# A decode block on one core: the first K in halves, longer weight runs, two quads of heads per PSUM bank, and y formed as rows

## The chip, the cores and the metric

The kernel runs on one core of a Trainium2 chip. The metric is the device time of one execution, in microseconds (us). Each kernel was run several times; the text quotes medians, and where the trace is read, the span of the profiled run (first to last instruction, about 1.8 us less than the device time).

## The reference, cut to what matters

One decode step for two sequences: layer norm, attention of 32 heads over a cache of 8,192 positions, a residual, a second layer norm, a gated MLP and another residual.

```python
# x [2,1,512]; k_cache, v_cache [2,32,8192,128]; wq [512,4096]; wo [4096,512]  (bf16)
q = layernorm(x) @ wq                              # 32 heads of 128
p = softmax(q . k * 128**-0.5);  o = p . v         # per head
h = x + o @ wo
g = layernorm(h) @ W_gate;  u = layernorm(h) @ W_up   # 512 -> 1376
h2 = h + ((g * (g > 0)) * u) @ W_down
```

K and V are 134 MB each; the weights are about 12.6 MB. The arithmetic is small, so the caches have to stream past once.

## The kernel before

A quad is four heads of one sequence; there are 16 quads. VectorE multiplies K with q and adds it up by halving, ScalarE makes the exponentials, TensorE multiplies them with V. K has a ring of two buffers and V one buffer, so a load can be issued only when its buffer has been read.

```python
def scores(n):                       # VectorE: one multiply, four halvings, one reduction
    nc.vector.tensor_tensor(out=kt, in0=kt, in1=q_broadcast, op=ALU.mult)
    ...
load_k(0); load_k(1); load_v(0)
for n in range(N - 1):
    scores(n)
    load_k(n + 2)                    # waits until scores(n) has read its buffer
    weighted_v(n)                    # TensorE
    load_v(n + 1)                    # waits until weighted_v(n) has read the buffer
# --- the end: wo, last V in four parts, gate, up (3/4 and 1/4), down
...
mlp_in(0, gate_ps, 0, KC)            # 44 matmuls of 2 columns
mlp_in(1, up_ps, 0, KC - 1)          # 33, need the first up transfer only
mlp_in(1, up_ps, KC - 1, KC)         # 11, need the second
...                                  # act = relu(gate) * up
for fc in range(FC):                 # y in columns: 44 matmuls of 2 columns
    for c in range(KC):
        nc.tensor.matmul(out=y_ps[:, c, :], lhsT=wd[:, fc][:, c * P:(c + 1) * P], rhs=act[:, fc, :], ...)
nc.vector.tensor_tensor(out=y, in0=y_ps, in1=hc, op=ALU.add)
...                                  # four transposes on TensorE, two copies, one output transfer
```

The softmax here doesn't subtract the row's maximum and nothing guards it: scores larger than these inputs give would overflow.

## Time and profile before

| | before |
|---|---|
| device time, median of 3 | 662.81 us |
| span of the profiled run | 660.9 us |
| bytes moved, share of the DMA engines' time in the kernel's queue | 281.28 MB, 98.9% |
| VectorE busy | 588.0 us (89%) |

The page of the kernel before, cut to its span, the busy times (us, share of the span, instructions), the kernel's queue (packets, MB, share of 16 engines' span) and the chain of waits:

```profile
span 660.9 us, 3558 instructions
...
PE 135.1 (20%) x1478; PEld 66.0 (10%) x1481; DVE 588.0 (89%) x139; ACT 74.4 (11%) x204; POOL 10.6 (2%) x51
...
q1 hardware_dynamic: 8244, 281.06, 98.9%
...
DVE 60%; DMA 36%; SPq 3%; issue 0%; PE 0%; DVEq 0%
```

Two engines look full. The queue is the one that is: VectorE still waits for K, while the queue holds its rate. The windows view has, for each stretch, the busy time and number of instructions of PE, PEld, DVE, ACT and POOL, then the granted clock, the DMA share and GB/s:

```profile
69.00:109.00 40.00, 7.83 (x72) 3.29 (x74) 39.76 (x8) 7.30 (x20) 0.00 (x0) 0.59 0.98 420
109.00:288.00 179.00, 35.40 (x365) 15.89 (x364) 177.77 (x32) 18.10 (x52) 0.00 (x0) 0.60 1.00 433
...
644.00:655.00 11.00, 8.57 (x171) 8.30 (x172) 2.04 (x14) 1.12 (x4) 0.00 (x0) 0.55 0.99 381
```

The stream runs at 433 GB/s in the middle. It is slower around the third K, at 69 to 109 us, and at the end, where the weights load.

Two lines of the timeline (start, duration, engine, line, operation) show why at 69 us: VectorE can start only when the whole first K has landed, and the third K is issued (SPq is the queue's issuing engine) only when the first has been read. By then the queue is nearly empty.

```profile
32.85 17.23 DVE L202 TENSOR_TENSOR k<-k,qrep 128x32768 bf16<-128x32768 bf16 x1 [23.45 <-DMA k<-in_A_k_cache_dram]
...
69.19 0.33 SPq L187 DMA_DIRECT2D k<-in_A_k_cache_dram  x1
```

The timeline of the end: the V matmuls of the second part of the last V, hd (h minus its mean), the up matmuls, act, the y matmuls in two lots, the last copy and the output:

```profile
642.62 1.26 PE L238 MATMUL o<-v,pm 128*16 128x512 bf16 x20 [1.96 <-DMA v<-in_A_v_cache_dram]
...
650.60 0.16 DVE L417 TENSOR_TENSOR hd<-hc,ln2mu 128x8 bf16<-128x8 f32 x1 [0.68 <-PE ln2mu L126]
...
652.83 1.71 PE L431 MATMUL up_ps<-hd,W 128*128 128x2 bf16 x44
...
654.58 0.24 DVE L452 TENSOR_TENSOR act<-gate,up_ps 96x2 bf16<-96x2 f32 x2 [0.94 <-PE up_ps L431]
...
654.87 0.57 PE L459 MATMUL y_ps<-act,W 128*128 128x2 bf16 x16 [0.33 <-DVE act L452]
...
656.24 1.09 PE L459 MATMUL y_ps<-act,W 128*128 128x2 bf16 x24 [0.80 <-DMA W<-in_B_W_down_dram]
...
658.38 0.41 DVE L476 CAST y_row<-yt_ps 2x256 bf16<-2x256 f32 x1 [0.75 <-PE yt_ps L470]
658.87 0.32 SPq L477 DMA_DIRECT2D out_dram<-y_row  x1
```

The gap between the two lots of y matmuls is a wait for W_down, as the view of waits says (who waited, for what, us, times, longest):

```profile
PE y_ps L459 <- DMA W<-in_B_W_down_dram: 0.8, 1, 0.8
```

### The profile page before, as it was taken

How to read it: one execution, taken by the hardware profiler on the slowest of the kernel's cores; microseconds unless marked ns; L12 is line 12 of the kernel's file. 1: busy time of each engine (PE TensorE's matmuls, PEld its weight loads, DVE VectorE, ACT ScalarE, POOL GpSimd, SP SyncE). 2: the span in 40 equal slices, each digit the busy share in tenths (PEclk: the TensorE clock that was granted, in tenths of full speed). 3: DMA queues.
4: the chain of work that ended last, by engine and by line, in shares of the span. 5: the costliest groups of instructions: out<-in, count | busy, mean ns of one | idle time of the engine just before them, and what ended most of it. 6: DMA issues, size and time to landing. Idle time of an engine off the chain costs nothing.

```text
span 660.9 us, 3558 instructions
## 1 busy us (share of the span) xinstructions
PE 135.1 (20%) x1478; PEld 66.0 (10%) x1481; DVE 588.0 (89%) x139; ACT 74.4 (11%) x204; POOL 10.6 (2%) x51
## 2 busy tenths in 40 slices
PE   2100402104040220304012030401204040130446
PEld 1000100001020010101001010100102010010215
DVE  1099999999999999999999998989899998999931
ACT  2100201010100101010102001010100101011020
POOL 6000000000000000000000000000000000000000
PEclk9755655757565575756657575565757556575765
DMA  9999999999999999999999999999999999999996
GB/s 381 444 444 440 386 444 440 441 444 405 428 437 441 440 409 433 445 432 436 440 420 429 444 425 436 440 424 432 429 436 436 440 425 437 424 428 440 400 410 251
DMA packets 8264, 281.28 MB, mean 426 GB/s; under 512 B 724, under 2 KB 1336, under 8 KB 3768
## 3 DMA queue, kind: packets, MB, share of 16 engines
q1 hardware_dynamic: 8244, 281.06, 98.9%
q8 instruction: 11, 0.18, 0.1%
q14 instruction: 5, 0.04, 0.0%
q10 hardware_dynamic: 4, 0.00, 0.0%
HBM read 281.05 MB, written 0.00 MB: 425 GB/s over the span
## 4 chain that ended last, share of the span: by engine, by line
DVE 60%; DMA 36%; SPq 3%; issue 0%; PE 0%; DVEq 0%
DMA k<-in_A_k_cache_dram 29%; DVE k L202 29%; DVE k L207 28%; DMA W<-in_A_wo_dram 5%; DVE sc L211 4%; SPq L364 3%; DMA W<-in_B_W_down_dram 2%; DVE ou L278 0%; DVE rep L275 0%; PE yt_ps L470 0%; PE y_ps L459 0%; DVE y_row L476 0%; SPq L119 0%; SPq L352 0%; DVEq L211 0%
## 5 line engine op out<-in xcount | busy, mean ns | idle before, releaser
L202 DVE TENSOR_TENSOR k<-k,qrep 128x32768 bf16<-128x32768 bf16 x16 | 275.5, 17220 | 37.1 <-DMA k<-in_A_k_cache_dram 37.1
L207 DVE TENSOR_TENSOR k<-k 128x16384 bf16<-128x16384 bf16 (+1 forms) x64 | 266.1, 4158 | 2.2
L238 PE MATMUL o<-v,pm 128*16 128x512 bf16 x1012 | 90.4, 535 | 489.0 <-DMA v<-in_A_v_cache_dram 435.6
L238 PEld LDWEIGHTS <-pm 128*16 128x16 bf16 x1012 | 33.1, 117 | 543.5 <-ACT pm L215 294.0
L215 ACT ACTIVATE pm<-sc 32x256 bf16<-32x256 f32 x64 | 49.2, 768 | 261.1 <-DVE sc L211 260.4
L246 ACT ACTIVATE osb<-o,turn_of 128x128 f32<-128x128 f32 x64 | 18.3, 368 | 293.9 <-PE o L238 287.2
L211 DVE TENSOR_REDUCE sc<-k 128x256 f32<-128x2048 bf16 x16 | 36.6, 2286 | 1.6
L268 PE MATMUL rep<-osb,head_of 128*128 128x128 f32 x112 | 17.8, 301 | 7.5 <-ACT osb L246 7.5
L268 PEld LDWEIGHTS rep<-osb,head_of 128*128 128x128 f32 x112 | 15.0, 188 | 14.5 <-ACT osb L246 14.5
L215 ACT ACTIVATION_READ_ACCUMULATOR pm<-sc 32x1 f32 x64 | 15.9, 249 | 0.0
L310 DVE RECIPROCAL zil<-zb 128x4 f32<-128x4 f32 x2 | 0.4, 179 | 12.9 <-PE zb L289 12.9
L169 PE MATMUL qps<-wq_sb,xnb 128*32 128x512 bf16 x64 | 5.4, 501 | 5.4 <-DMA wq_sb<-in_A_wq_dram 5.4
L229 PE MATMUL o<-zero 128*128 128x512 bf16 x14 | 5.5, 395 | 0.0
L388 PE MATMUL ar_ps<-W,oc 128*2 128x512 bf16 x28 | 3.2, 626 | 10.1 <-DVE oc L305 10.1
L92 POOL TENSOR_SCALAR_AFFINE_SELECT head_of<-head_of 128x128 f32<-128x128 f32 x16 | 5.0, 312 | 0.1
L431 PEld LDWEIGHTS <-W 128*128 128x128 bf16 (+1 forms) x88 | 3.8, 126 | 0.3 <-issue 0.3
L169 PEld LDWEIGHTS <-xnb 128*32 128x32 bf16 x64 | 2.6, 115 | 7.8 <-issue 6.1
L175 ACT ACTIVATE qrep<-qps 128x512 bf16<-128x512 f32 x4 | 2.4, 597 | 6.7 <-PE qps L169 6.7
L92 POOL TENSOR_SCALAR_AFFINE_SELECT turn_of<-turn_of 128x4 f32<-128x4 f32 x16 | 3.1, 191 | 0.0
L278 DVE TENSOR_REDUCE ou<-rep 128x16 f32<-128x512 f32 (+1 forms) x4 | 2.5, 624 | 0.1
L464 DVE TENSOR_TENSOR y<-y_ps,hc 128x8 bf16<-128x8 f32 x1 | 0.2, 167 | 2.7 <-PE y_ps L459 2.7
L275 DVE TENSOR_TENSOR rep<-rep,pick 128x512 f32<-128x512 f32 (+1 forms) x4 | 2.5, 622 | 0.0
(87 smaller groups left out, 45.9 us busy)
## 6 DMA issues: line engine op xcount, KB each, us to landing
wq_sb<-in_A_wq_dram SPq DMA_DIRECT2D x1, 4096.0 KB, 12.8
v<-in_A_v_cache_dram SPq DMA_DIRECT2D x1, 4096.0 KB, 14.6
W<-in_A_wo_dram SPq DMA_DIRECT2D x1, 3584.0 KB
v<-in_A_v_cache_dram SPq DMA_DIRECT2D x1, 2560.0 KB, 20.4
W<-in_B_W_gate_dram SPq DMA_DIRECT2D x1, 1376.0 KB, 26.3
W<-in_B_W_up_dram SPq DMA_DIRECT2D x1, 1032.0 KB, 28.4
v<-in_A_v_cache_dram SPq DMA_DIRECT2D x1, 1024.0 KB, 22.4
W<-in_B_W_down_dram SPq DMA_DIRECT2D x2, 512.0 KB, 20.5
```

The costliest lines, as they stand in the source:

```text
L92: nc.gpsimd.affine_select(out=t, in_=t, compare_op=ALU.not_equal, fill=1.0, base=-(Q * g + base), pattern=pat, channel_multiplier=1)
L169: nc.tensor.matmul(out=qps[h * Q:(h + 1) * Q], lhsT=xnb[:, c, b, :], rhs=wq_v[:, c, g:g + QP, h, :], start=(c == 0), stop=(c == KC - 1),)
L202: nc.vector.tensor_tensor(out=kt, in0=kt, in1=_view(qrep[:, b, i, :], 0, [[0, T], [1, Dh]]), op=ALU.mult)
L207: nc.vector.tensor_tensor(out=kt[:, :, 0:half], in0=kt[:, :, 0:half], in1=kt[:, :, half:width], op=ALU.add)
L211: nc.vector.tensor_reduce(out=sc, in_=kt[:, :, 0:8], axis=AXIS.X, op=ALU.add)
L215: nc.scalar.activation(out=pm[ps, :, h], in_=sc[ps, :], func=ACT.Exp, accum_out=(zm[ps, b, i:i + 1] if i < LQ else zl[ps, b, h:h + 1]), sc ...
L229: nc.tensor.matmul(out=o, lhsT=_view(zero, 0, [[0, P]]), rhs=_view(zero, 0, [[0, TG * Dh]]), start=True, stop=False, skip_group_check=True)
L238: nc.tensor.matmul(out=o[g:g + G * TG], lhsT=pm[:, ts, :].rearrange("p t h -> p (t h)"), rhs=vt[:, ts, :].rearrange("p t d -> p (t d)"), s ...
L246: nc.scalar.activation(out=osb[:, t, :], in_=o[:, t * Dh:(t + 1) * Dh], func=ACT.Copy, scale=turn_of[:, t:t + 1])
L268: nc.tensor.matmul(out=reps[i // HQ][:, i % HQ, :], lhsT=head_of.rearrange("k h m -> k (h m)"), rhs=osb[:, t, :], start=(t == 0), stop=(t ...
L364: nc.sync.dma_start(out=wd_sb[:, f:f + r, :].rearrange("p r n -> p (r n)"), in_=B_W_down[f * P:(f + r) * P, :].rearrange("(p r) n -> p (r ...
L431: nc.tensor.matmul(out=ps[0:w, fc, :], lhsT=lhsT, rhs=hd[:, c, :], start=(c == 0 and fc == 0), stop=(c == KC - 1), skip_group_check=True)
```

## The change

Its intent: (1) the first K comes in two transfers, so VectorE starts earlier; (2) wo, gate and up are laid out so that each partition reads one long run; (3) two quads share a PSUM bank, which halves the evictions and repetitions and needs no clearing matmuls; (4) y is formed as rows in two column groups of TensorE (partitions 0 and 32, 256 columns each), so there are no transposes. The residual and the wo product go into the same rows. (5) GpSimd no longer builds the masks. The diff, cut to its core:

```diff
-    pms = [consts.tile([P, T, G], bf16, name=f"pm{i}") for i in range(NM)]
+    pm = consts.tile([P, R + NG * W2], bf16)        # 16 columns of data, 16 of zeros, in turn
-    for g in range(P // Q): ... nc.gpsimd.affine_select(...)   # masks on GpSimd
+    build_masks()                                   # reductions of the identity on VectorE
 ...
-            nc.tensor.matmul(out=o[g:g + G * TG], lhsT=pm[:, ts, :], ..., start=False, ...)
+            nc.tensor.matmul(out=o[g:g + W2],
+                             lhsT=_view(pm, (0 if lane else R) + t // TG * W2, [[1, W2]]),
+                             ..., start=(first and k < P // Q), ...)
 ...
-    load_k(0)
+    HALVES = (0, T // 2, T)
+    load_k(0, HALVES)
 ...
-    nc.sync.dma_start(out=wo_sb..., in_=A_wo[...].rearrange("(i p j) n -> p i (j n)", p=P, j=J))
+    for k, n in enumerate(SIZES):                   # 4, 2, 1 quads: runs of 16, 8, 4 KB
+        nc.sync.dma_start(out=wo_sb[...], in_=A_wo[r0:...].rearrange("(p j) n -> p (j n)", p=P))
 ...
-    for g, w, c0, c1 in ((0, B_W_gate, 0, KC), (1, B_W_up, 0, KC - 1), (1, B_W_up, KC - 1, KC)):
-        nc.sync.dma_start(..., in_=w.rearrange("(c p) n -> p c n", p=P)[:, c0:c1, :])
+    for g, w in ((0, B_W_gate), (1, B_W_up)):
+        nc.sync.dma_start(..., in_=w.rearrange("(p c) n -> p (c n)", c=KC))
 ...
+    def y_rows(lhsT, rhs, first=False, last=False):
+        for e in range(2):
+            nc.tensor.matmul(out=y_ps[e * Q:e * Q + m], lhsT=lhsT, rhs=rhs[:, e * HD:(e + 1) * HD], ...)
 ...
     for fc in range(FC):
-        for c in range(KC): nc.tensor.matmul(out=y_ps[:, c, :], ...)
-    ... add, transposes, two copies, one output transfer
+        y_rows(act[0:w, fc, :], (wd_sb[:, fc, :] if fc < NF else wd_l[0:w]), last=(fc == FC - 1))
+    nc.vector.tensor_copy(y_row, y_ps[0:2 * Q])
+    for e, eng in ((0, nc.sync), (1, nc.scalar)):
+        eng.dma_start(out=..., in_=y_row[e * Q:e * Q + B, :])
```

Two smaller edits are not in this cut: the last V is cut at 7/8 instead of 13/16 (so its second part is 24 matmuls instead of 20), and x for the residual comes by a small transfer on the other queue.

## The prediction

> **What bounds the kernel now.** The DMA queue. The page's queue part gives 281.28 MB and 98.9% of the span of 16 engines. In the trace's packet records a 65,536-byte packet takes 2,419 ns; sixteen at once make 433.5 GB/s, and the windows view shows 433 GB/s in each middle stage. The Trainium skill, "DMA: Bandwidth & Descriptors", section "Where 436 GB/s comes from", puts the ceiling at 435 GB/s; this trace agrees. 281.28 MB at 433.5 is 648.9 us of a 660.9 us span. VectorE is busy 588 us (89%) but has slack: it waits for K in nine places, 37.1 us.
>
> **Where the other 12 us are** (cumulative packet bytes against 433.5 GB/s): 2.6 us before the stream is up; 0.55 us at 69 to 80 us, where K2 is issued (69.19) just as the queue runs empty, because its buffer comes free only when VectorE has done K0; about 0.8 us of slow drift; 0.9 us while wo loads (4 KB packets: 164 ns, 400 GB/s); 1.1 us while gate, up and down load (2,752-byte packets: 113 ns, 390 GB/s); then about 6 us from the last packet (655 us) to the end: landing, the last y matmuls (656.95), y, transposes, y_row (658.79), output DMA (2.1 us).
>
> **What the change does.**
> 1. First K in halves: VectorE starts near 23 us instead of 32.85, K2 is issued near 60 us, the 0.55 us bubble goes. The other 9 us are not on the path: VectorE will only wait more for later K (waits for K rise from 37 to near 37, moved from the start to the middle).
> 2. wo in 16/8/4 KB runs: estimate -0.5 us. gate/up in 11,008-byte runs: estimate -0.6 us, both from the packet durations by size. (Same page, "Why small descriptors are slow": a fixed overhead per packet; here about 12 ns.)
> 3. Shared PSUM bank, no clears, 56 instead of 112 rep matmuls, half the evictions: PE and ACT work hidden behind DMA: 0. One pm instead of two: exp of quad n+1 must follow V matmuls of quad n, which end 8 to 11 us earlier: 0.
> 4. Final part: the last-V chain loses six f32 matmuls (L405: 1.85 us to about 0.45) but gains y_rows(wol) (8 matmuls of 256 columns) ahead of mu and nine small DVE operations. I put act at 653.5 (was 654.8), still ahead of the last W_down landing (655.3, was 656.95), so DMA ends the chain. After it: three pairs of 256-column y matmuls (0.6 us), one copy (0.45), output DMA: 1.3 us instead of 1.85 from landing to DMA issue.
>
> Sum: -0.55 -0.5 -0.6 -0.55 = -2.2 us, about 0.3%.
>
> **Predicted: 660.6 us, 80% range 659.4 to 662.2. Faster by over 2%: 0.02; within 2%: 0.97; slower by over 2%: 0.01.**
>
> **What would show it.** Step 1: K2 issue near 60 us, no dip at 70 us, DVE's first multiply near 23 us. Step 2: at least 420 GB/s at 615 to 655 us, last packet near 653.3. Step 3: PE busy down by 15 us or more with no change in K to K spacing (38.7 us). Step 4: the chain still ends in DMA W_down, then y_ps, y_row copy, output.
>
> **What would make it wrong.** If the pairs of y matmuls at partitions 0 and 32 do not overlap, 22 of them at the granted clock of 0.5 take 4.7 us and the end is no earlier. If PE's work before V's last parts (ar, f32 y rows) runs past their landing, the compute chain ends last. If long rows do not speed packets, 1.1 us stay. If the V14 to V15 hand-over (about 3 us of queue left at 621.8) gets later, the queue runs dry.

## The result

The changed kernel took 661.62 us (median of 5, 661.4 to 661.99) against 662.67 (median of 5) for the kernel before: ratio 0.9985, 95% interval 0.9973 to 0.9997. Ratios here are the mean time of one kernel's runs over that of the other's of the same rounds, so not quite the ratio of the quoted medians. It is 1.05 us less, inside the predicted range, and half of the 2.2 us that the prediction had as its sum.

The page after, the same parts:

```profile
span 659.8 us, 3322 instructions
...
PE 126.5 (19%) x1390; PEld 64.0 (10%) x1391; DVE 592.1 (90%) x180; ACT 64.0 (10%) x175; POOL 2.5 (0%) x8
...
q1 hardware_dynamic: 7124, 281.06, 98.8%
...
DMA 77%; PE 15%; another core or an unknown queue 8%; issue 0%; DVE 0%; ACT 0%; ACTq 0%
```

(The chain now runs through V and TensorE; followed back from the end, it passes through the wait for up.) The bottleneck is the same queue with the same bytes. TensorE is busy 8.6 us less and ScalarE 10.4 us less, which bought nothing that the middle shows; the windows there have the same 433 GB/s:

```profile
69.00:109.00 40.00, 5.62 (x64) 2.46 (x64) 39.76 (x7) 2.97 (x8) 0.00 (x0) 0.59 0.98 423
109.00:288.00 179.00, 31.66 (x344) 14.59 (x343) 171.00 (x33) 18.20 (x52) 0.00 (x0) 0.59 1.00 433
```

Short windows can mislead, because a packet's bytes are booked where it starts. For a finer account I added up the packets of the kernel's queue over time (each packet's bytes spread over its duration) and read when a given amount had passed. In order of the queue, 264.2 MB is the end of the fifteenth V, 268.4 that of wo, 276.8 that of the last V, 279.6 that of up; the total is 281.05.

| passed | before | after | after minus before |
|---|---|---|---|
| 28.0 MB | 67.29 | 67.32 | +0.03 |
| 31.0 MB | 74.75 | 74.24 | -0.51 |
| 100 MB | 234.60 | 233.78 | -0.82 |
| 264.2 MB | 613.87 | 613.10 | -0.77 |
| 268.3 MB | 624.05 | 622.88 | -1.17 |
| 276.8 MB | 644.13 | 642.99 | -1.14 |
| 279.6 MB | 651.12 | 649.72 | -1.40 |
| 281.0 MB | 655.57 | 654.24 | -1.33 |

So the stream gained 1.33 us: 0.54 at the third K (from +0.03 to -0.51), about 0.3 between 31 and 100 MB and nothing more up to 264 MB, 0.40 at wo and 0.26 at gate and up; 0.07 was lost again at W_down. The first step looks as predicted, VectorE 10 us earlier and the third K issued at 60 us:

```profile
22.86 8.69 DVE L215 TENSOR_TENSOR k<-k,qrep 128x16384 bf16<-128x16384 bf16 x1 [11.06 <-DMA k<-in_A_k_cache_dram]
...
60.23 0.33 SPq L193 DMA_DIRECT2D k<-in_A_k_cache_dram  x1
```

The end, the lines that answer to those of before (the add and the transposes are gone):

```profile
643.21 1.48 PE L250 MATMUL o<-v,pm 128*32 128x512 bf16 x24 [1.20 <-DMA v<-in_A_v_cache_dram]
...
649.01 0.16 DVE L488 TENSOR_TENSOR hd<-hc,ln2mu 128x8 bf16<-128x8 f32 x1 [0.53 <-PE ln2mu L133]
...
652.48 1.74 PE L505 MATMUL up_ps<-hd,W 128*128 128x2 bf16 x44 [1.11 <-DMA W<-in_B_W_up_dram]
654.26 0.24 DVE L523 TENSOR_TENSOR act<-gate,up_ps 96x2 bf16<-96x2 f32 x2 [2.22 <-PE up_ps L505]
...
654.55 2.30 PE L456 MATMUL y_ps<-W,act 128*2 128x256 bf16 x20 [0.33 <-DVE act L523]
656.64 0.42 PE L456 MATMUL y_ps<-wd_l,act 96*2 96x256 bf16 x2
657.11 0.42 DVE L530 CAST y_row<-y_ps 64x256 bf16<-64x256 f32 x1 [2.61 <-PE y_ps L456]
657.55 0.32 SPq L532 DMA_DIRECT2D out_dram<-y_row  x1
```

There is no wait for W_down any more. There is a new one, for up:

```profile
PE up_ps L505 <- DMA W<-in_B_W_up_dram: 1.1, 1, 1.1
```

Act is ready at 654.50 (654.26 + 0.24; 654.82 before), although hd was 1.6 us earlier. All 22 y matmuls come after act and take 2.5 us (654.55 to 657.06). The output is issued 1.32 us earlier (657.55 against 658.87), and then takes 2.29 us to the end of the span where it took 2.06: two transfers on two queues instead of one. That gives the 1.09 us by which the spans differ.

### The profile page after: what moved, and what is told of

Same layout as the page of the kernel before. It is cut to its first block, busy times and chain, and to the rows that moved or that the text cites. A ratio compares the mean times of both kernels' runs of the same rounds, so it can differ in the third digit from the quotient of the medians.

```text
span 659.8 us, 3322 instructions
## 1 busy us (share of the span) xinstructions
PE 126.5 (19%) x1390; PEld 64.0 (10%) x1391; DVE 592.1 (90%) x180; ACT 64.0 (10%) x175; POOL 2.5 (0%) x8
## 4 chain that ended last, share of the span: by engine, by line
DMA 77%; PE 15%; another core or an unknown queue 8%; issue 0%; DVE 0%; ACT 0%; ACTq 0%
DMA v<-in_A_v_cache_dram 70%; PE o L250 13%; DMA W<-in_B_W_up_dram 4%; DMA wq_sb<-in_A_wq_dram 2%; DMA W<-in_A_x_dram 1%; PE qps L175 1%; PE y_ps L456 0%; PE up_ps L505 0%; DVE y_row L530 0%; DVE act L523 0%; ACT osb L260 0%; ACTq L260 0%
## 5 line engine op out<-in xcount | busy, mean ns | idle before, releaser
L215 DVE TENSOR_TENSOR k<-k,qrep 128x32768 bf16<-128x32768 bf16 (+1 forms) x17 | 275.7, 16218 | 33.1 <-DMA k<-in_A_k_cache_dram 33.1
L221 DVE TENSOR_TENSOR k<-k 128x16384 bf16<-128x16384 bf16 (+3 forms) x68 | 266.8, 3923 | 2.3
L250 PE MATMUL o<-v,pm 128*32 128x512 bf16 x1016 | 90.9, 535 | 500.1 <-DMA v<-in_A_v_cache_dram 500.1
L250 PEld LDWEIGHTS <-pm 128*32 128x32 bf16 x1016 | 38.6, 129 | 550.3 <-issue 381.7
L227 ACT ACTIVATE pm<-sc 32x256 bf16<-32x256 f32 x64 | 47.2, 737 | 346.6 <-DVE sc L224 345.3
L224 DVE TENSOR_REDUCE sc<-k 128x256 f32<-128x2048 bf16 (+1 forms) x17 | 36.7, 2160 | 2.0 <-DVE k L221 0.5
L260 ACT ACTIVATE osb<-o,turn_of 128x128 f32<-128x128 f32 x36 | 10.3, 368 | 210.5 <-PE o L250 210.5
L296 PE MATMUL rep<-osb,spread 128*64 128x128 f32 (+1 forms) x64 | 9.9, 297 | 3.9 <-ACT osb L260 3.9
L296 PEld LDWEIGHTS rep<-osb,spread 128*64 128x64 f32 (+1 forms) x64 | 7.3, 161 | 8.7 <-ACT osb L260 7.8
L456 PE MATMUL y_ps<-W,act 128*2 128x256 bf16 x20 | 2.3, 415 | 0.3 <-DVE act L523 0.3
## 6 DMA issues: line engine op xcount, KB each, us to landing
wq_sb<-in_A_wq_dram SPq DMA_DIRECT2D x1, 4096.0 KB, 12.3
```

The lines of the kernel that those rows point to most:

```text
L215: nc.vector.tensor_tensor(out=kp, in0=kp, in1=_view(qrep[:, b, i, :], 0, [[0, hi - lo], [1, Dh]]), op=ALU.mult)
L221: nc.vector.tensor_tensor(out=kp[:, :, 0:half], in0=kp[:, :, 0:half], in1=kp[:, :, half:width], op=ALU.add)
L224: nc.vector.tensor_reduce(out=sc[:, lo:hi], in_=kp[:, :, 0:8], axis=AXIS.X, op=ALU.add)
L227: nc.scalar.activation(out=p_of[ps, :, :, h], in_=sc[ps, :].rearrange("p (g t) -> p g t", t=TG), func=ACT.Exp, accum_out=(zm[ps, b, i:i + ...
L250: nc.tensor.matmul(out=o[g:g + W2], lhsT=_view(pm, (0 if lane else R) + t // TG * W2, [[1, W2]]), rhs=vt[:, t:t + TG, :].rearrange("p t d ...
L260: nc.scalar.activation(out=osb[:, t, :], in_=o[:, t * Dh:(t + 1) * Dh], func=ACT.Copy, scale=turn_of[:, t:t + 1])
```

## The experiments

The first theory (A): the single transfer of up holds back the end. The rivals: (B) the stream's last packet decides, (C) the y matmuls decide. The runs were made in three calls, and each call has its own runs of the kernel before beside it; its medians were 662.49, 662.64 and 662.73. The changed kernel itself was run again only in the third (e11_same_again), so a comparison of the first two calls with its 661.62 is across calls, and a difference of 0.2 us there means nothing.

### e1_up_split: up in two transfers again

```diff
-    for g, w in ((0, B_W_gate), (1, B_W_up)):
+    for g, w, c0, c1 in ((0, B_W_gate, 0, KC), (1, B_W_up, 0, KC - 1), (1, B_W_up, KC - 1, KC)):
-                          in_=w.rearrange("(p c) n -> p (c n)", c=KC))
+                          in_=w.rearrange("(p c) n -> p (c n)", c=KC)[:, c0 * F:c1 * F])
```

> The changed kernel with up loaded in two transfers (three quarters of its rows per partition, then the last quarter), as before.py did. Theory A (the single up transfer gates the final chain: its landing at 652.43 us held the up matmuls back 1.1 us, while gate was done at about 650.9): up starts near 651.4, act near 653.5, the 22 y matmuls then meet the landing of the last W_down rows at about 656; y_row copy starts near 656.4 instead of 657.11, span about 0.7 us shorter (659.1), time about 660.9. Rival B (the end is set by the data stream, whose last packet ends at 655.4, not by up): the wait on up goes but a wait on W_down of about the same length appears, span within 0.2 us of 659.8. Rival C (the y matmuls are slow by themselves): y starts earlier but nothing else moves, so the end follows act, about 1.0 us earlier.

661.9 us, no gain. The timeline of its end:

```profile
643.12 2.75 PE L250 MATMUL o<-v,pm 128*32 128x512 bf16 x24 [0.87 <-DMA v<-in_A_v_cache_dram]
...
650.75 0.16 DVE L488 TENSOR_TENSOR hd<-hc,ln2mu 128x8 bf16<-128x8 f32 x1 [1.08 <-PE ln2mu L133]
...
657.58 0.42 DVE L530 CAST y_row<-y_ps 64x256 bf16<-64x256 f32 x1 [2.61 <-PE y_ps L456]
```

No wait for up or W_down is left. But the V matmuls took 2.75 us instead of 1.48, hd came 1.7 us later, and the up matmuls started 0.5 us later than with the wait. The y_row copy comes later too, at 657.58. The granted clock was 0.5 in that stretch where the profile of the changed kernel had 1.0. None of the three theories had this. So this profile does not decide between them. The five times of this kernel fall in two groups: 661.36 and 661.41, and 661.9 to 662.24. The spread is larger than that of the changed kernel. That suggests that with the wait gone the clock shows in the time. The record has the mean granted clock of every run over its whole span: 0.598 and 0.593 in the two fast ones, 0.581 to 0.586 in the other three, which fits. It is a hint and no proof: in e4_y_cols, below, the two runs with the highest mean clock were the slowest, and only one run of each kernel has a trace.

### e2_k_whole: the first K in one transfer again

```diff
-    HALVES = (0, T // 2, T)
+    HALVES = (0, T)
```

> The changed kernel with the first K in one transfer again. If the bubble explanation holds: K2 is issued near 69 us, the stream loses about 0.5 us between 28 and 34 MB, VectorE's first multiply starts near 32 us, and everything later, the end included, is about 0.5 us later (span 660.3, time about 662.1). If the half transfers are worth the whole of VectorE's earlier start (9 us), it would be several us later. If they are worth nothing, no shift in the times at which given amounts of bytes have passed.

661.51 us (661.49 to 661.61): nothing is lost. The expectation failed, and the trace shows why:

```profile
32.32 17.22 DVE L215 TENSOR_TENSOR k<-k,qrep 128x32768 bf16<-128x32768 bf16 x1 [20.70 <-DMA k<-in_A_k_cache_dram]
...
68.66 0.33 SPq L193 DMA_DIRECT2D k<-in_A_k_cache_dram  x1
```

The first K lands 0.53 us earlier than in the kernel before (32.32 against 32.85), so the third K is issued at 68.66 instead of 69.19, and the pass from 28 to 31 MB takes 7.11 us (7.46 before, 6.92 with halves). The stream passes 281.0 MB at 654.28, as with halves (654.24). So in the changed kernel the halves are worth 0.19 us in the place and nothing at the end; something else in the change had mended most of the bubble (0.35 of 0.54 us).

A candidate is in the packet records: in the profile of before, an 8,192-byte packet of an instruction queue ran at 12.4 us for 309 ns on one of the engines. No profile of a kernel of the changed family has it. Around 31 us the sixteen engines start their 65,536-byte packets up to 860 ns apart in before and 551 ns here. The difference is just those 309 ns, and a transfer counts as landed only when all sixteen engines are done (the Trainium skill, "DMA: Bandwidth & Descriptors", section "Why a DMA increments its semaphore by 16 and not by 1", says that only the full count of 16 means that all data has landed). VectorE's start, 0.53 us apart with the stream only 0.10 us apart at 12.5 MB, agrees.

### e9_pool_masks: did the GpSimd instructions cause that packet?

```diff
     nc.gpsimd.memset(pm, 0.0)
+    for g in range(16):
+        for wide in (P, TG, B):
+            nc.gpsimd.affine_select(out=pm[:, 0:wide], in_=pm[:, 0:wide], ..., fill=0.0, ...)
```

(First K whole, as in e2_k_whole.)

> The changed kernel with the first K whole (as e2_k_whole) and 48 GpSimd selects of the size of those that the change removed, which here rewrite zeros. Open: why the bubble at 69 to 80 us went although the first K was whole. Theory D: the removed GpSimd mask building caused the 8,192-byte instruction packet at 12.4 us, seen in the profile of before alone; it delayed one of the 16 engines, so the first K landed later (VectorE from 32.85 us; 32.32 in e2_k_whole), K2 was issued later and the queue ran dry longer. Then this run shows that packet near 12 us, VectorE from about 32.7, K2 issued near 69.1 and 31.0 MB at about 74.7 us. Rival: the packet comes by chance or from another part; then 32.3, 68.7 and 74.3 as in e2_k_whole.

One look (a single run, 662.46 us, whose state is unknown, so its time is not compared): no packet near 12 us, VectorE from 32.38, third K at 68.72, 31.0 MB at 74.42. Theory D falls. What brings that packet in the kernel before stays open.

### e10_before_halves: the halves alone, in the kernel before

The same edit to loads and scores as in the change, nothing else.

> The kernel before, with the first K in two halves as the only change. The prediction's step 1 says: K2 issued near 60 us, 28 to 31 MB passes in 6.95 us instead of 7.46, everything later is 0.5 us earlier, and since the chain of before ends in the landing of W_down, the end too: span 660.4, time 662.1 beside 662.6. Rival: the compute chain from the last V ends as late as the stream, and the end moves by less than 0.2.

662.04 us against 662.73, ratio 0.9992 (0.9979 to 1.0004). The interval contains 1, so the time alone does not show a gain; the trace has to.

```profile
60.46 0.33 SPq L187 DMA_DIRECT2D k<-in_A_k_cache_dram  x1
```

The packet is there again (12.3 us), and does little harm: VectorE's first multiply starts at 23.10 us (22.86 in the changed kernel, without the packet) and the third K is issued at 60.46. The pass from 28 to 31 MB takes 6.92 us, as predicted for this step, and 281.0 MB have passed at 654.82 (655.57 before). The span is 660.2 against 660.9. So the prediction's step 1 is right as a mechanism, and in the kernel before the stream and the span of these two profiles are 0.75 us earlier (the medians differ by 0.7). About 0.3 us of it came only between 31 and 100 MB, for which I have no cause. In the changed kernel the same step is worth nothing, because the lateness that it cures was mostly gone.

### e6_short_runs: the short packets on the new layout

```diff
+        for u in range(n):                     # wo in seven transfers, runs of 4 KB
-                          in_=w.rearrange("(p c) n -> p (c n)", c=KC))
+        for c in range(KC):                    # gate, up: runs of 2,752 bytes
```

> The changed kernel with wo loaded in seven transfers with runs of 4 KB per partition and gate and up in eight transfers with runs of 2,752 bytes, so the packets of the kernel before on the layout of the changed one. If packet size is what the longer runs bought: about 0.4 us more between 264.2 and 268.3 MB and 0.3 to 0.5 us more between 276.8 and 279.6 MB. If the times at those bytes stay within 0.1 us, the gain there had another cause. The end need not move as much, because up now comes in four pieces and the chain from V to y may end last: span 659.8 to 660.7.

661.95 us; span of the profile 659.9. The time in the queue for these bytes:

| stretch | before | after | e6_short_runs |
|---|---|---|---|
| 264.2 to 268.3 MB (wo) | 10.18 | 9.78 | 10.07 |
| 276.8 to 279.6 MB (gate, up) | 6.99 | 6.73 | 6.99 |

The run length is worth 0.29 us at wo and 0.26 at gate and up. The remaining 0.11 at wo has another cause. The end of this profile:

```profile
643.36 1.48 PE L250 MATMUL o<-v,pm 128*32 128x512 bf16 x24 [1.92 <-DMA v<-in_A_v_cache_dram]
...
PE y_ps L459 <- DMA W<-in_B_W_down_dram: 0.7, 2, 0.4
```

The stream is 0.5 us later at 281.0 MB (654.72) and the span is the same (659.9 against 659.8): the clock was granted (1.48 us for the V matmuls), up, here in four pieces, was not waited for, act was ready at 653.94, 0.56 us earlier than in the changed kernel, the y matmuls waited 0.7 us for W_down, and the y_row copy started at 657.06 against 657.11. So in this profile half a microsecond of stream was not seen in the end: with the wait for up gone, the landing of W_down, here later, became the wait, as in the kernel before. This profile is of the fastest of four runs (661.65), and the median is 0.33 us above the changed kernel's; I do not call the late stream free.

### e3_y_one_group: do the pairs of y matmuls overlap?

```diff
-            nc.tensor.matmul(out=y_ps[e * Q:e * Q + m], ...)
+            nc.tensor.matmul(out=y_ps[0:m, e, :], ...)       # both halves at partition 0
```

> The changed kernel with both halves of the y rows in the same output partitions (one column group of the array) instead of partitions 0 and 32. If the pairs overlapped in the changed kernel: 22 matmuls of 256 columns at the granted clock of 0.5 now take about 4.7 us instead of 2.5, the copy reads 512 instead of 256 elements per partition (about 0.75 us instead of 0.42), so the end is about 2.5 us later (span 662.3, time 664). If they did not overlap, the y matmuls stay at 2.5 us and only the copy adds 0.35.

```profile
654.25 4.43 PE L456 MATMUL y_ps<-W,act 128*2 128x256 bf16 x20 [0.33 <-DVE act L523]
658.47 0.63 PE L456 MATMUL y_ps<-wd_l,act 96*2 96x256 bf16 x2
```

The y matmuls take 4.85 us (654.25 to 659.10) instead of 2.5, and the time is 663.84 us, ratio 1.0019 to the kernel before. So the pairs at partitions 0 and 32 do run side by side; without that the change would be slower than the kernel it replaces (the longer copy, 0.68 instead of 0.42 us, is only a small part of the 2.2 us lost).

### e4_y_cols: y in columns again

```diff
-        y_rows(act[0:w, fc, :], ...)
+        for c in range(KC): nc.tensor.matmul(out=y_ps[:, c, :], lhsT=columns(wd)[:, c, :], rhs=act[0:w, fc, :], ...)
+    ... y = y_ps + hc; four transposes; two copies; one output transfer
```

> The changed kernel with y formed as columns again (44 matmuls of 2 columns, add of h, four transposes, two copies), everything else kept. If rows are worth what the traces suggest (from act to the issue of the output 3.97 us before, 3.03 after, of which before spent some waiting for W_down): the y matmuls are short but wait for the last W_down rows near 656, then add, transposes and copies take 1.4 us, output issued near 657.9 instead of 657.55: span 0.2 to 0.6 us longer, one output transfer instead of two perhaps 0.2 us shorter. If rows were the main gain of the change: about 1 us longer. The y-row matmuls before mu are gone too; if these delayed the chain, gate starts earlier by up to 0.5 us.

662.1 us, 0.5 us more than the changed kernel's 661.62.

The line of the output's issue:

```profile
658.24 0.32 SPq L534 DMA_DIRECT2D out_dram<-y_row  x1
```

From act (654.90) to the output's issue it takes 3.34 us, against 3.05 with rows; the single output then takes 2.07 us instead of 2.29. From act to the end that is 5.41 against 5.34 us: in these traces rows gain 0.07 us after act and no more. The rest of the half microsecond is that act comes 0.40 us later, in a profile where the V matmuls took 2.75 us, so at another clock. What rows are worth in time is therefore not shown.

### e5_y_four_groups: y rows in four column groups

```diff
-    HD = D // 2
+    HD = D // 4          # e = 0..3, partitions 0, 32, 64, 96; copy of 128 x 128; two outputs of four partitions
```

> The changed kernel with the y rows in four column groups of 128 columns (44 matmuls at partitions 0, 32, 64, 96) instead of two of 256. If column groups overlap, as theory says: 44 matmuls cost what 44 two-column matmuls cost in these traces, about 1.7 us against 2.5, and the copy 128 elements per partition, about 0.25 against 0.42. The end comes 0.7 to 1.0 us earlier than in the changed kernel (span 658.9, time 660.8), unless the last W_down rows, which land near 656.1, become the wait; then 0.5 us. Rival: the landing of W_down already decides, and nothing moves.

661.29 us (661.06 to 661.4), ratio 0.9976.

```profile
654.52 1.58 PE L457 MATMUL y_ps<-W,act 128*2 128x128 bf16 x40 [0.33 <-DVE act L524]
...
656.26 0.29 DVE L531 CAST y_row<-y_ps 128x128 bf16<-128x128 f32 x1 [1.79 <-PE y_ps L457]
```

The y matmuls take 1.7 us (654.52 to 656.21) and the copy 0.29, as expected: the copy starts 0.85 us earlier than in the changed kernel although act was no earlier. This is theory C's answer: what comes after act is fully exposed. The rival falls, because the landing of W_down did not hold it. But the output, issued at 656.57, now takes 2.93 us to the end of the span, 0.64 more than with two halves, which gives most of the gain back.

### e7_warm: extra TensorE work to keep the clock

```diff
-    clear(ar_ps)
+    for _ in range(40):
+        clear(ar_ps)
```

> The changed kernel with 39 extra matmuls of zeros (512 columns) while TensorE waits for VectorE's normalisation, from about 622 to 632 us, off the critical path. Theory: the chain from the last V to mu is TensorE work whose speed depends on the granted clock, and the clock's windows fall differently from run to run (1.0 from 638.5 to 648.7 in the profile of the changed kernel, 636.8 to 643.7 with the whole first K, where the V matmuls took 2.15 instead of 1.48 us). With the extra work the clock is 1.0 from before 632 to at least 644 us, the V matmuls after the wait take about 1.5 us, mu is ready near 648.9, and the runs spread less. The end then waits for up as in the profiled run: span 659.6 to 659.9, time about 661.5. If the clock has no part in it, the same as the changed kernel with the same spread.

662.1 us: a miss. The clock records show 1.0 from 619.7 to 643.6 and 0.5 from then on, so most of the V matmuls that were to profit missed it:

```profile
639.74 0.63 PE L457 MATMUL y_ps<-ar,row_of 128*32 128x256 f32 x4
...
643.22 2.40 PE L250 MATMUL o<-v,pm 128*32 128x512 bf16 x24 [2.85 <-DMA v<-in_A_v_cache_dram]
```

Between these two lines TensorE has nothing to do for 2.85 us, and the clock was lost just as the V matmuls began. That the gap did it is not shown, and its length is no rule: e6_short_runs kept the clock at 1.0 through a gap of 1.92 us before the same V matmuls, and e11_same_again, next, lost it at 642.8 with a gap of only 0.48.

### e11_same_again: the changed kernel, unchanged

> The changed kernel once more, not one character different. Theory: the windows of the granted clock are not tied to the program, so their edges in this profile lie elsewhere (638.5 and 648.7 before), the V matmuls after the last wait take between 1.5 and 2.8 us, act is ready between 653.7 and 654.8, and the end follows act by about the same 5.3 us. If the windows are tied to the program, edges and times repeat to 0.2 us.

661.55 us. The same program, another profile:

```profile
642.96 2.75 PE L250 MATMUL o<-v,pm 128*32 128x512 bf16 x24 [0.48 <-DMA v<-in_A_v_cache_dram]
...
650.17 0.16 DVE L488 TENSOR_TENSOR hd<-hc,ln2mu 128x8 bf16<-128x8 f32 x1 [0.67 <-PE ln2mu L133]
...
652.66 1.75 PE L505 MATMUL up_ps<-hd,W 128*128 128x2 bf16 x44
```

The windows view of 643 to 645 us, first for the changed kernel's first profile, then for this one (clock 1.00 against 0.50, third number from the end):

```profile
643.00:645.00 2.00, 1.79 (x28) 0.96 (x27) 0.18 (x1) 0.00 (x0) 0.00 (x0) 1.00 1.00 416
```

```profile
643.00:645.00 2.00, 2.00 (x20) 0.81 (x23) 0.00 (x0) 0.00 (x0) 0.00 (x0) 0.50 1.10 457
```

The clock's windows lie elsewhere: 1.0 from 638.5 to 648.7 in the first profile, and from 639.4 to 642.8 and 646.2 to 649.6 here. The V matmuls take 2.75 instead of 1.48 us, hd is 1.16 us later, and yet act is only 0.19 later (654.69) and the span 0.2 longer. The reason is the two walls: with the clock the up matmuls wait for the landing of up at 652.4, without it TensorE itself comes to them hardly earlier (it waits 0.2 us for up and starts at 652.66). So theory A is half of the answer. The wait is real, but without the clock there is almost nothing to gain by taking it away. That e1_up_split gains where the clock is granted fits its two fast runs and the early act of e6_short_runs (653.94), but no profile of e1_up_split itself shows it.

### e8_four_split and e12_all: versions that should beat both

e8_four_split takes four groups, up in two, and half of the y-row matmuls of the last heads after mu.

```diff
-    for h in range(G): y_rows(ol[:, h, :], wol[:, h, :])
+    for h in range(G // 2): y_rows(ol[:, h, :], wol[:, h, :])
     mu = centred(hc, "ln2")
+    for h in range(G // 2, G): y_rows(ol[:, h, :], wol[:, h, :])
```

> Four column groups, up in two transfers, and half of the y-row matmuls of the last heads after mu instead of before it. Theory: the final compute chain ends last, not the data stream; each of its steps shortened shows until W_down's landing near 656.1 is reached. Expected: y matmuls 1.7 us, act between 653.4 (clock granted) and 654.5 (not), y_row copy start between 656.3 and 656.5, span 658.7 to 659.1, time 660.4 to 660.9. If the stream decides: span stays at 659.8 with a wait on W_down of about a microsecond.

661.33 us, no faster than e5_y_four_groups alone and slower than the 660.4 to 660.9 expected. Its clock was not granted for the V matmuls (2.75 us), and its last copy starts at 656.14, the earliest of all runs, with the output issued at 656.46:

```profile
656.14 0.29 DVE L533 CAST y_row<-y_ps 128x128 bf16<-128x128 f32 x1 [1.70 <-PE y_ps L457]
```

e12_all adds four dummy matmuls in the wait before the last V parts, meant to keep the clock, and sends the output as four transfers of two rows.

```diff
     y_rows(row_of, ar, first=True)
+    for _ in range(4):
+        clear(ar_ps)
 ...
+    for e, eng in enumerate((nc.sync, nc.scalar, nc.sync, nc.scalar)):
+        eng.dma_start(out=..., in_=y_row[e * Q:e * Q + B, :])
```

> As e8_four_split (up in two, four column groups, y rows of the last heads split around mu) with output in four transfers of two rows each instead of two of four, and four 512-column matmuls of zeros in the wait before the last V parts[...]. Expected: V matmuls after the wait about 1.5 us, act before 653.6; the y matmuls then wait for W_down, which lands near 655.7, and y_row starts near 656.0 (656.14 in e8_four_split). Output issue to end 2.6 us instead of 2.9. Span 658.7 to 659.1, time about 660.8, the fastest so far. If the output needs 2.9 us whatever its form, span 659.2. If the dummy matmuls come in the way (clock not granted), as e8_four_split or 0.5 us later.

660.98 us (660.9 to 661.04), ratio 0.9974 (0.996 to 0.9987) against the kernel before: the fastest version, 0.6 us below the changed kernel in medians, and their ranges do not touch (661.4 was the least of both sets of the changed kernel).

```profile
643.11 2.64 PE L250 MATMUL o<-v,pm 128*32 128x512 bf16 x24 [1.35 <-DMA v<-in_A_v_cache_dram]
...
656.28 0.29 DVE L535 CAST y_row<-y_ps 128x128 bf16<-128x128 f32 x1 [1.60 <-PE y_ps L457]
656.60 0.61 SPq L537 DMA_DIRECT2D out_dram<-y_row  x2
```

The dummies did not do what they were for. The V matmuls still took 2.64 us, since the clock dropped at 643.3, and nothing waited for W_down. The gain over e8_four_split is in the output: 2.61 us from issue to end instead of 2.91.

## Why the prediction was right or wrong

Its time (660.6, range 659.4 to 662.2) held the measured 661.62, and "within 2%" was right, but its sum was twice the effect.

- **The bound: right.** The queue, before and after, 433 GB/s in the middle of both.
- **Step 1, halves of the first K, -0.55 us: the mechanism right, the attribution wrong.** The 0.51 us appeared at the place foretold and the third K was issued at 60.2 us. But the changed kernel has most of it (0.35 of 0.54 us, counted from 28 MB) with a whole first K too (e2_k_whole); alone in the kernel before the halves earn all of it (e10_before_halves). The prediction took the late landing at 32.85 us as given; the rest of the change had moved it to 32.32, by a way that stays open. That the stream gained at this place in the changed kernel is so no proof of step 1: the number came right by another road. VectorE's other 9 us were worth nothing, as predicted: its waits for K fell only from 37.1 to 33.1 us.
- **Step 2, long runs, -1.1 us: mis-sized.** Measured -0.66 (0.40 and 0.26), of which run length is 0.55. The estimate took the packets' durations as their cost. But in this trace consecutive short packets overlap: 1,024 packets of 113.2 ns on 16 engines add up to 7.25 us, while 2.80 of their 2.82 MB passed in 6.99. The long ones hardly do: the 256 packets of 11,008 bytes add up to 6.74 us, and 2.80 MB passed in 6.73.
- **Step 3, TensorE and ScalarE work: right that it is worth nothing.** The middle's rate did not change. The sign it gave, 15 us less of TensorE, was too much; it was 8.6, because the V matmuls stay and are 91 us either way.
- **Step 4, the end, -0.55 us: the step that failed.** It put act at 653.5 with W_down as the last wall, and so only three pairs of y matmuls after it. Act was at 654.50 and 654.69 in two profiles of the changed kernel. W_down was not waited for at all, and all eleven pairs, 2.5 us, came after act. Part of the step held: the f32 matmuls shrank as foreseen (1.85 to 0.38 us) and hd came 1.6 us earlier. But I had read from the diff that up now lands whole, and had not asked when: in the first profile that wait took 1.11 us back. And the sum has no term for the granted clock, on which the V matmuls took 1.48 us in one profile of this kernel and 2.75 in the other. In its place the runs show a compute chain of about 5.3 us from act to the end of the span that nothing hides, with two walls before it at almost the same time. The output, taken as unchanged at 2.1 us, took 2.29.
- **Not foreseen:** about 0.3 us gained between 31 and 100 MB, which e10_before_halves has as well. Most of it lies in one place: 82 to 86 MB took 9.51 us in the kernel before and 9.23 in the changed one. Its cause is open, and as the kernel before has one trace, it may be chance of that run.

The sum in the terms of the spans: stream -1.33 (predicted -1.65), output issued 1.32 us earlier, so nothing from step 4 (predicted -0.55), output +0.23 (predicted 0), together -1.09. This is book-keeping: that the output's issue moved by as much as the stream is no sign that the stream still decides the end, since W_down is no longer waited for.

## What to carry to other kernels

A stream that fills the queue hides everything but its two ends, so read the last wait and count what must still be done after it; here 5 us of small TensorE work, a copy and an output of 2 to 3 us decided more than all the TensorE and ScalarE work saved in the middle. When several transfers become one, ask who was content with the first of them. And when a part of a change seems to explain a gain, take that part alone out of the new kernel and into the old one: both answers were needed here, and they differed.

## What the Trainium skill lacked or had wrong

- "TensorE: Matmul & The Clock Gate", sections "Part 1: The HAM clock gate" and "HAM oscillation — how this bites in real kernels": its free-running window of 3,413 ns agrees with these traces, where stretches of clock 1.0 last 3.4, 6.8 or 10.2 us (23.9, seven windows, in e7_warm) and lie differently in two profiles of one program (edges at 638.5 and 648.7, or 639.4, 642.8, 646.2 and 649.6). It advises "no PE-idle gaps >~3.4µs"; here the clock was lost with gaps of 2.85 us (e7_warm, at 643.6), 1.35 us (e12_all, at 643.3) and 0.48 us (e11_same_again, at 642.8), and kept with one of 1.92 us (e6_short_runs). So staying under 3.4 us was not enough, and the length of the gap does not sort these runs; what does stays open.
- The same page does not say which matmuls count as activity: at 650 to 652 us of the kernel before TensorE was busy 1.75 of 2 us with two-column matmuls, at clock 0.50. In e11_same_again it was busy 3.08 of 3.40 us from 639.4 to 642.8 and lost the clock; in e6_short_runs 1.48 of 3.40 us from 641.1 to 644.5, and kept it.
- "DMA: Bandwidth & Descriptors", section "Where 436 GB/s comes from": its fabric ceiling of 435 GB/s agrees with the measured 433.5. The page gives no figure for how far the packets of one engine overlap: for those of 2,752 bytes 7.25 us added up and 6.99 passed.
- The same page lacks what a small output costs by its form. From issue to the end of the span: one transfer of 2 rows of 1,024 bytes 2.06 us; two of 2 rows of 512 bytes on two queues 2.29; four of 2 rows of 256 bytes 2.61; two of 4 partitions of 256 bytes 2.91 to 2.93.
- No page that I used gives what an instruction packet costs the landing of a transfer beside it: one of 8,192 bytes took 309 ns, and with the first K whole the spread of the engines after it was 860 ns with the packet (before) and 551 ns without (e2_k_whole). With the first K in halves it was 751 ns with the packet (e10_before_halves) and 708 without (the changed kernel), so the cost is not a fixed one.
